# Attention over pooled keys and a gated MLP on one core: exp, pooling and filler products of the first phase rearranged

## The chip, the core and the metric

One core of a Trainium2 chip runs the whole program. Its engines are TensorE (PE, matrix products; PEld is its weight load), VectorE (DVE), ScalarE (ACT), GpSimd (POOL) and SyncE (SP), which here only issues transfers. Each engine works through its own instruction list in order and waits on semaphores. The metric is the device time of one execution in microseconds (us); the time before is the median of three.

## The reference

For each of 8 batches and 8 heads (576 tokens, 64 numbers a head) keys and values are averaged over groups of 8 tokens, so that 72 are left; then softmax attention, and the heads side by side are the rows x of a gated MLP:

```python
k_p = k.reshape(B, H, Sp, pool, D).mean(axis=3)      # Sp = 72, pool = 8
v_p = v.reshape(B, H, Sp, pool, D).mean(axis=3)
scores = scale * np.matmul(q, k_p.transpose(0, 1, 3, 2))
attn = np.exp(scores - np.max(scores, axis=-1, keepdims=True))
attn = attn / (np.sum(attn, axis=-1, keepdims=True) + 1e-09)
x = heads side by side of np.matmul(attn, v_p)       # 4608 x 512
xn = x / rms * rms_g                                 # rms over the 512
g = xn @ w_gate; val = xn @ w_val                    # 512 x 1536 each
out = (g * sigmoid(g) * val) @ w_out                 # 1536 x 512
```

The weights come as 64-bit numbers; the kernel converts them itself.

## The kernel before

Heads are taken in pairs (p = 0 to 3 in each batch b), tokens of the MLP in 9 blocks of 512, the 1536 inner columns in 12 pieces f. A 32-bit number is split into a high and a low part of a shorter format, and a product of two numbers is made of three: high by high, high by low, low by high. So a block needs 12 x 36 = 432 products of 128 x 128 by 512.

**The later phase** (blocks 1 to 8) is plain code: while PE works on block i, the attention of the batch after it is made a step at a time. Its first step takes the first pair of batch 2: k is loaded, summed over the groups by DVE (`s_kpool`), and only then q, since both use one buffer; then `s_heads` makes the scores.

**The first phase** makes batches 0 and 1, converts all weights, and runs block 0. Its order is the string `ORDER`: each word is a step with its indices, called in turn, and so the order of every engine's list. The steps that matter here, with the letter in the string: k, q, v load a pair; K and V sum keys and values over groups on DVE; S makes a pair's scores `pss` (two heads, five tiles each); M takes the row maxima of a head and multiplies them by minus the scale; E makes the exponentials, five ACT instructions for a head with the sum of a row as a second result; R makes the inverse of the sums; N multiplies on POOL; T transposes on PE into `pst`, C and D copy that (DVE, ACT); A is the product with the values, `psx`, X and Y copy it (DVE, ACT); Z squares it, P sums squares by PE (`psr`), p adds those up (`total`), r takes the root, s the inverse, B spreads it (`psb`), I makes the scaled x, x and y its high and low part (`xh`, `xl`). l loads a piece of weights, a (ACT), b, c, d (DVE: shift, `w_low`, sign) convert it, h (ACT) and w or W (DVE or POOL) split it. g and e are the gate and value products of a piece f (`mm1`, tile `psg`), G, F, i, j or L the steps between (`gate` on ACT, `val` on DVE, `act_hi` on ACT, `act_lo` on DVE or POOL), o the output products (`mm2`, tile `po`). z is `warm`, 16 products of the identity with itself, once, at the start.

The split of block 1's x (`split_x(1)`: for each of four pieces two ACT and two DVE instructions) follows behind the string. The last output products of block 0 copy their result to `o`, and SP sends it out; k and v of batch 2 stand behind those in SP's list.

## Time and profile before

| | |
|---|---|
| time, median of 3 runs (range) | 1046.81 us (1045.53 to 1047.74) |
| profiled execution, and its span | 1049.04 us, 1047.3 us |
| PE busy, products | 1026.6 us, 98% |
| DVE, ACT, POOL busy | 506.3, 416.6, 115.9 us (48%, 40%, 11%) |
| mean granted clock of TensorE | 0.98 of full (full is 2.4 GHz, 0.5 is 1.2 GHz) |

The time of the profiled execution is 1.7 us more than its span, which goes from the first to the last instruction. PE counts as busy from a product's start to its modelled end, also when it runs at half clock, so the shares are read stretch by stretch.

### The profile page before, as it was taken

The page shows a single profiled execution, that of the slowest core. Times are in us where ns is not written, and L with a number is a line of the kernel's source. Part 1 is how long each engine was busy: PE and PEld are TensorE (multiplying, and loading weights), DVE is VectorE, ACT ScalarE, POOL GpSimd, SP SyncE. Part 2 cuts the span into 40 slices and gives each one's busy share as a digit, 9 for nine tenths or more (in the row PEclk, how much of TensorE's full clock was granted, in tenths as well). Part 3 has the DMA queues.
Part 4 walks back from the last instruction along what each step waited for, and adds up shares of the span by engine and source line. Part 5 has one row for each costly group of instructions (what it writes and reads, how often), then busy time and mean ns, then how long its engine had stood idle before and what let it go on. Part 6 is the DMA issues. An engine that isn't in the chain of part 4 may idle for free.

```text
span 1047.3 us, 13134 instructions
## 1 busy us (share of the span) xinstructions
PE 1026.6 (98%) x4994; PEld 816.2 (78%) x4994; DVE 506.3 (48%) x857; ACT 416.6 (40%) x771; POOL 115.9 (11%) x108
## 2 busy tenths in 40 slices
PE   7899998999999999999999999999999999999998
PEld 6677776777877777777877787778777888888886
DVE  6799985635455446344653455445452431122112
ACT  5767664433443345333533354335342431121111
POOL 2313430111001100111001101110011000000000
PEclk8599999999999999999999999999999999999999
DMA  9445412222022201221122103210210010001001
GB/s 292 133 163 177 170 62 72 74 76 74 25 73 73 58 25 50 77 66 36 43 75 54 57 3 108 55 53 12 88 36 14 1 41 1 1 1 41 1 1 40
DMA packets 38702, 65.44 MB, mean 62 GB/s; under 512 B 6384, under 2 KB 20208, under 8 KB 37360
## 3 DMA queue, kind: packets, MB, share of 16 engines
q1 hardware_dynamic: 38640, 64.61, 20.3%
q8 instruction: 39, 0.64, 0.3%
q14 instruction: 23, 0.19, 0.1%
HBM read 47.19 MB, written 9.44 MB: 54 GB/s over the span
## 4 chain that ended last, share of the span: by engine, by line
PE 88%; DVE 5%; DMA 2%; ACT 2%; issue 1%; SPq 0%; ACTq 0%
PE psg L490 53%; PE po L521 27%; PE pss L282 4%; PE psx L343 3%; DVE wt L140 1%; DMA wx<-w 1%; DVE wt L144 1%; DMA main<-kT 1%; DVE wt L136 1%; ACT prob L260 1%; PE psr L412 1%; DVE w L162 0%; PE pst L323 0%; PE psb L436 0%; DMA q<-qT 0%
## 5 line engine op out<-in xcount | busy, mean ns | idle before, releaser
L490 PE MATMUL psg<-xh,w 128*128 128x512 f32 x1728 | 541.3, 395 | 2.9 <-ACT xh L462 2.9
L490 PEld LDWEIGHTS psg<-xh,w 128*128 128x128 f32 x1728 | 322.3, 189 | 82.9 <-ACT xraw L350 3.4
L490 PE MATMUL psg<-xl,w 128*128 128x512 f32 x864 | 338.2, 392 | 0.0
L521 PE MATMUL po<-w,hh 128*128 128x512 f32 x864 | 223.3, 395 | 0.0
L502 DVE TENSOR_TENSOR act<-act,psg 128x512 f32<-128x512 f32 x108 | 73.6, 682 | 288.1 <-PE psg L490 254.5
L521 PEld LDWEIGHTS po<-w,hh 128*128 128x128 f32 x864 | 162.6, 188 | 37.7
L490 PEld LDWEIGHTS psg<-xl,w 128*128 128x128 f32 x864 | 162.6, 188 | 35.5 <-DVE xl L463 0.7
L506 ACT CAST hh<-act 128x512 fp32r<-128x512 f32 x108 | 67.1, 622 | 212.5 <-DVE act L502 212.4
L497 ACT ACTIVATE act<-psg 128x512 f32<-128x512 f32 x108 | 64.5, 597 | 204.8 <-PE psg L490 202.6
L521 PE MATMUL po<-w,hl 128*128 128x512 f32 x432 | 122.4, 395 | 0.4 <-DVE hl L510 0.4
L521 PEld LDWEIGHTS po<-w,hl 128*128 128x128 f32 x432 | 79.5, 188 | 20.3 <-DVE act L502 2.0
L510 DVE TENSOR_TENSOR hl<-act,hh 128x512 fp32r<-128x512 f32 x102 | 70.0, 686 | 40.9 <-ACT hh L506 38.5
L299 POOL TENSOR_TENSOR prob<-prob,sm 128x360 f32<-128x360 f32 x48 | 38.7, 826 | 446.2 <-DVE sm L297 257.9
L497 ACT ACT_TABLE_LOAD x40 | 51.3, 1283 | 47.8 <-PE psg L490 26.6
L291 DVE TENSOR_REDUCE mx<-pss 128x5 f32<-128x360 f32 x48 | 23.4, 528 | 49.8 <-PE pss L282 49.6
L304 DVE STREAM_TRANSPOSE sq<-prob 128x960 f32<-128x960 f32 x24 | 28.3, 1179 | 38.8 <-POOL prob L299 34.6
L384 POOL TENSOR_TENSOR acc<-acc,sq 128x576 f32<-128x576 f32 x21 | 30.7, 1461 | 146.4 <-ACT sq L378 146.4
L239 DVE TENSOR_REDUCE pv<-v 72x128 f32<-72x1024 f32 x28 | 34.0, 1214 | 22.8 <-PE psx L343 21.5
L282 PEld LDWEIGHTS pss<-pk,q 64*128 64x128 f32 x560 | 34.5, 193 | 12.0 <-issue 8.9
L282 PE MATMUL pss<-pk,q 64*128 64x72 f32 x560 | 38.6, 283 | 1.8 <-DVE own L329 0.9
L294 ACT ACTIVATE prob<-prob 128x360 f32<-128x360 f32 x48 | 23.1, 505 | 31.9 <-DVE prob L293 31.8
L343 PE MATMUL psx<-pt,pv 72*64 72x256 f32 (+2 forms) x224 | 35.4, 429 | 0.0
(90 smaller groups left out, 701.2 us busy)
## 6 DMA issues: line engine op xcount, KB each, us to landing
wx<-w SPq DMA_DIRECT2D x10, 1024.0 KB
v<-vN SPq DMA_DIRECT2D x32, 288.0 KB
out<-o SPq DMA_DIRECT2D x36, 256.0 KB
wx<-w SPq DMA_DIRECT2D x16, 512.0 KB
k<-kT SPq DMA_DIRECT2D x28, 288.0 KB
q<-qT SPq DMA_DIRECT2D x28, 288.0 KB
pt<-sq SPq DMA_DIRECT2D x96, 40.0 KB
pt<-sq SPq DMA_DIRECT2D x96, 32.0 KB
```

The source lines that it names most:

```text
L239: nc.vector.tensor_reduce(pv, s["v"], AX.X, ALU.add)
L282: nc.tensor.matmul(s["ps", h][:, t * SP:(t + 1) * SP], s["q"][r, o:o + P], s["pk"][r, :], start=True, stop=True)
L299: nc.gpsimd.tensor_tensor(pr, pr, sm[:, :, None].broadcast_to(shape), ALU.mult)
L304: nc.vector.transpose(sq.rearrange("p b g j -> p g b j"), prob.rearrange("p g (b j) -> p g b j", b=3))
L343: nc.tensor.matmul(ps[r, :n], s["pv"][:, r], s["pt"][:, h, tok], start=True, stop=True)
L384: nc.gpsimd.tensor_add(acc[b], acc[b], st[b, p]["sq"])
L490: nc.tensor.matmul(ps[:, :NB], w[:, c, cols], x[c], start=(j == 0), stop=(j == len(todo) - 1))
L497: nc.scalar.activation(t, ps[:, :NB], AF.Silu)
L502: nc.vector.tensor_mul(t, t, ps[:, :NB])
L506: nc.scalar.copy(a, st["act"])
L510: eng.tensor_sub(l, st["act"], hh[i, f].bitcast(F32))
L521: nc.tensor.matmul(po[i][t], x[i, f][:, t * P:(t + 1) * P], w, start=(f == 0 and k == 0), stop=(f == NF - 1 and k == 2))
```

## The change

- `warm` multiplies `ones` (the short format) by itself, into one fixed bank. It stands at three places: 35 products at the start, 5 behind the first scores, 28 ahead of the first `psb`.
- The values of batch 0 are loaded in another layout (`v0`, tokens down) and summed over groups by five products with a 0/1 matrix `group` (`s_vpool0`, `psv`), then copied once. The four DVE sums of batch 0's values go.
- Four of the eight sums of keys in the first phase go to POOL, as three adds each (step %).
- For 12 of the 16 early heads the exponentials are made as in the later phase: DVE subtracts the maximum (u), ACT makes the exponentials of the whole head in one instruction (f), DVE sums (n). The other four heads keep E; for those pairs ACT multiplies the pooled keys by minus the scale (~), so that M is one minimum. The product of the maximum with the scale goes for all 16.
- For batch 1 the sums of both heads are scaled by ACT and inverted in one instruction.
- `ORDER` is another string; which steps of the weights and the activations go to POOL changes with it (w and W, j and L).
- `split_x(1)` (step O) stands in the string, ahead of the last `val`.

```diff
-zg:0 k01 q00 k00 v00 q01 v01 q02 k02 v03 K01 v02 k03 q03 l3 l1 l0 K00 l2 l5 S00:01 V00 k10 q10 S01:45 M000 M001 E000
+zz k01 k00 q00 q02 k02 q01 U0 U1 q03 K01 U2 k03 l3 %00 l0 l1 l5 l2 ~00 k10 S00:01 q10 K02 M001 z5 S02:45 M000 E001
...
-Fa B11:1 H10 ia o9 H11 gb:2 La eb:3 Gb oa Fb ib jb ob k20 v20
+ea:3 Ga bo co hp do wp ho o9 Fa Wo ia gb:2 La eb:3 Gb oa O1 Fb ib jb ob k20 v20
...
+    group = const.tile([P, 2 * SP - 8], F32, name="group")
+    nc.vector.memset(group, 0.0)
+    nc.vector.tensor_reduce(group[:, 64:80], ident.rearrange("p (s o) -> p s o", o=POOL), AX.X, ALU.add)
...
+    def load_v0(i):
+
+        if i < 2:
+            v = st["v0", i] = space2(NF - 1 - i, [P, 2, DM], F32, f"v0_{i}")
+            nc.sync.dma_start(v, v0[i * 2 * P:(i + 1) * 2 * P].rearrange("(t p) n -> p t n", p=P))
+        else:
+            v = st["v0", 2] = space2(NF - 3, [P, 2, DM], F32, "v0_2")
+            nc.sync.dma_start(v[:S - 4 * P, 0, :], v0[4 * P:])
+
+    def s_vpool0(t):
+
+        if t == 0:
+            st["pv0"] = bank(0, "psv")
+        n = min(P, S - t * P)
+        nc.tensor.matmul(st["pv0"][:SP, :], group[:n, 64 - 16 * t:64 - 16 * t + SP], st["v0", t // 2][:n, t % 2, :],
+                         start=(t == 0), stop=(t == 4))
...
+        if pool:
+            for w in (4, 2):
+                nc.gpsimd.tensor_add(k[:, :, :w], k[:, :, :w], k[:, :, w:2 * w])
+            nc.gpsimd.tensor_add(pk, k[:, :, 0], k[:, :, 1])
+        else:
+            nc.vector.tensor_reduce(pk, k, AX.X, ALU.add)
...
+    def s_negate(b, p):
+
+        st[b, p]["neg"] = True
+        nc.scalar.mul(st[b, p]["pk"], st[b, p]["pk"], -EXP_SCALE)
...
-        nc.vector.tensor_reduce(mx, s["ps", h][:, :n * SP].rearrange("p (t k) -> p t k", k=SP), AX.X, ALU.max)
-        nc.vector.tensor_scalar(mx, mx, -EXP_SCALE, None, ALU.mult)
+        nc.vector.tensor_reduce(mx, s["ps", h][:, :n * SP].rearrange("p (t k) -> p t k", k=SP), AX.X,
+                                ALU.min if "neg" in s else ALU.max)
...
+    def s_less(b, p, h):
+
+        s, n = st[b, p], len(OFFS2)
+        nc.vector.tensor_tensor(
+            probs(b, p, h), s["ps", h][:, :n * SP].rearrange("p (t k) -> p t k", k=SP),
+            s["mx"][:, h, :, None].broadcast_to([P, n, SP]), ALU.subtract)
+
+    def s_plain(b, p, h):
+
+        pr = probs(b, p, h)
+        nc.scalar.activation(pr, pr, AF.Exp, scale=EXP_SCALE)
+
+    def s_sum(b, p, h):
+        nc.vector.tensor_reduce(st[b, p]["sm"][:, h, :], probs(b, p, h), AX.X, ALU.add)
...
-        ps = bank(0, "warm")
         for _ in range(n):
-            nc.tensor.matmul(ps[:, :P], ident, ident, start=True, stop=True)
+            nc.tensor.matmul(st["warm"][:, :P], ones, ones, start=True, stop=True)
 
     with tc.manual_schedule(engines=ENGINES):
         first_phase()
-        split_x(1)
```

Where it moves instructions: PE's list between the last sums of squares and the first gate product, before (`pst`, `psx` of batch 1's first pair around `psb`) and then of the change.

```order
L412 MATMUL psr_339<-one,own_119 116x1 x5
L323 MATMUL pst_0_0_494<-ident,prob 72x128 x4
L436 MATMUL psb_0_505<-ident,r_491 128x116 x3
L436 MATMUL psb_0_505<-ident,r_491 128x112
L436 MATMUL psb_0_505<-ident,r_491 128x52
L436 MATMUL psb_1_517<-ident,r_491 128x64
L323 MATMUL pst_0_2_520<-ident,prob 72x128 x2
L323 MATMUL pst_0_1_524<-ident,prob 72x128 x4
L343 MATMUL psx_0_0_541<-pt_0_493,pv_0_438 64x288 x2
L343 MATMUL psx_0_1_550<-pt_0_493,pv_0_438 64x288 x2
L490 MATMUL psg_0_0_564<-xh_0_546,w_0_384 128x512 x2
```

```order
L473 MATMUL psr_364<-one,own_176 116x1 x5
L656 MATMUL warm<-ones 128x128 x28
L497 MATMUL psb_0_551<-ident,r_508 128x116 x3
L497 MATMUL psb_0_551<-ident,r_508 128x112
L497 MATMUL psb_0_551<-ident,r_508 128x52
L497 MATMUL psb_1_561<-ident,r_508 128x64
L384 MATMUL pst_0_0_565<-ident,prob 72x128 x4
L384 MATMUL pst_0_1_578<-ident,prob 72x128 x4
L384 MATMUL pst_0_2_587<-ident,prob 72x128 x2
L343 MATMUL pss_1_0_591<-pk_1_457,q_1_472 128x72
L343 MATMUL pss_1_1_592<-pk_1_457,q_1_472 128x72
```

The filler products stand ahead of `psb`. Behind the last row come eight more scores of the second pair (`pss_1`) and then `psg`; `psx` of the first pair stands behind the first gate product's twelve.

DVE's list at the end of block 0, before and of the change: `act_11` is `val(11)`, `hl_11` its low part, `xl` the low parts of block 1's x.

```order
L502 TENSOR_TENSOR act_11_1509<-act_11_1509,psg_11_1_1496 128x512
L510 TENSOR_TENSOR hl_11_1526<-act_11_1509,hh_11_1524 128x512
L527 COPY o_0_1531<-po_0_656 128x512
L527 COPY o_2_1543<-po_2_658 128x512
L463 SCALAR_TENSOR_TENSOR xl_0_1560<-xraw_297,gcol,xh_0_1556 128x64
L463 SCALAR_TENSOR_TENSOR xl_0_1560<-xraw_540,gcol,xh_0_1556 128x448
L463 SCALAR_TENSOR_TENSOR xl_1_1561<-xraw_297,gcol,xh_1_1557 128x64
```

```order
L563 TENSOR_TENSOR act_10_1473<-act_10_1473,psg_10_1_1460 128x512
L524 SCALAR_TENSOR_TENSOR xl_0_1545<-xraw_340,gcol,xh_0_1541 128x64
L524 SCALAR_TENSOR_TENSOR xl_0_1545<-xraw_638,gcol,xh_0_1541 128x448
L524 SCALAR_TENSOR_TENSOR xl_1_1546<-xraw_340,gcol,xh_1_1542 128x64
L524 SCALAR_TENSOR_TENSOR xl_1_1546<-xraw_638,gcol,xh_1_1542 128x448
L524 SCALAR_TENSOR_TENSOR xl_2_1547<-xraw_340,gcol,xh_2_1543 128x64
L524 SCALAR_TENSOR_TENSOR xl_2_1547<-xraw_638,gcol,xh_2_1543 128x448
L524 SCALAR_TENSOR_TENSOR xl_3_1548<-xraw_340,gcol,xh_3_1544 128x64
L524 SCALAR_TENSOR_TENSOR xl_3_1548<-xraw_638,gcol,xh_3_1544 128x448
L563 TENSOR_TENSOR act_11_1527<-act_11_1527,psg_11_1_1514 128x512
L571 TENSOR_TENSOR hl_11_1568<-act_11_1527,hh_11_1566 128x512
L588 COPY o_0_1573<-po_0_717 128x512
```

The eight `xl` stood behind the copies of the output and now stand ahead of `val(11)`.

DVE's list at the first maxima, of the change: `sm` rows are sums and their inverse.

```order
L281 TENSOR_REDUCE mx_2_216<-pss_2_1_187 128x5
L298 TENSOR_TENSOR main_131<-pss_2_1_187,mx_2_216 128x360
L281 TENSOR_REDUCE mx_2_216<-pss_2_0_186 128x5
L298 TENSOR_TENSOR main_131<-pss_2_0_186,mx_2_216 128x360
L281 TENSOR_REDUCE mx_1_225<-pss_1_1_205 128x5
L298 TENSOR_TENSOR main_126<-pss_1_1_205,mx_1_225 128x360
L322 TENSOR_SCALAR sm_0_179<-sm_0_179 128x5
L323 RECIPROCAL sm_0_179<-sm_0_179 128x5
L281 TENSOR_REDUCE mx_1_225<-pss_1_0_204 128x5
L298 TENSOR_TENSOR main_126<-pss_1_0_204,mx_1_225 128x360
L308 TENSOR_REDUCE sm_2_217<-main_131 128x5
L322 TENSOR_SCALAR sm_2_217<-sm_2_217 128x5
```

Before, each maximum was followed by its product with the scale, and there was neither the subtraction into `main` nor a sum on DVE.

## Rows read from the trace of the kernel before

**Rows 1.** The page's first line.

```profile
span 1047.3 us, 13134 instructions
```

**Rows 2.** Busy time by engine in stretches: start:end, length, then PE, PEld, DVE, ACT and POOL busy us with instruction counts, mean granted clock of TensorE (1 is full), DMA share, GB/s. The first stretch goes from the first row maximum to the last of the four `first_x` products, the second from there to the last piece of converted weights.

```profile
9.56:52.95 43.39, 36.33 (x217) 26.84 (x217) 34.69 (x78) 33.39 (x138) 13.82 (x13) 0.62 0.65 211
52.95:161.20 108.25, 103.56 (x511) 80.47 (x511) 102.24 (x136) 72.33 (x150) 35.75 (x22) 0.98 0.41 138
```

**Rows 3.** The chain of work that ended last, in order of time, some pieces of 0 to 190 us: start, length, what (x: instructions in the piece).

```profile
22.52 1.52 ACT main L260 x10
...
35.79 4.04 PE psx L343 x16
39.83 5.91 PE psr L412 x30
...
45.76 0.18 DVE total L417
...
47.82 2.82 PE psb L436 x12
...
55.12 12.12 PE psg L490 x48
...
182.37 4.02 DMA q<-qT
...
186.52 1.34 PE pss L282 x20
```

**Rows 4.** The view of Rows 2, one microsecond to a row; the third figure from the end is the granted clock.

```profile
12.00:13.00 1.00, 0.00 (x0) 0.00 (x0) 0.23 (x2) 0.64 (x6) 0.00 (x0) 0.94 1.08 242
...
57.00:58.00 1.00, 1.00 (x5) 0.82 (x4) 0.96 (x3) 0.98 (x3) 0.03 (x1) 0.88 0.63 168
...
180.00:181.00 1.00, 1.00 (x4) 0.77 (x3) 1.00 (x5) 0.95 (x3) 0.00 (x0) 0.56 1.01 301
```

**Rows 5.** Instructions in order of time in 0 to 60 us: start, length, engine, line, operation, tiles, count; in brackets the idle time before it and what ended it.

```profile
1.35 6.07 PE L593 MATMUL warm<-ident 128*128 128x128 f32 x32 [1.35 <-POOL ident masks.py:199]
...
9.56 0.52 DVE L248 TENSOR_REDUCE mx<-pss 128x5 f32<-128x360 f32 x1
...
18.39 2.41 PE L282 MATMUL pss<-own,main 64*128 64x72 f32 x20
...
20.73 2.35 PE L323 MATMUL pst<-ident,main 128*72 128x128 f32 x10
...
28.43 1.07 POOL L272 TENSOR_TENSOR main<-main,sm 128x360 f32<-128x360 f32 x1 [0.39 <-ACT own L329]
...
52.78 1.14 ACT L474 CAST xh<-xraw 128x512 fp32r<-128x512 f32 x2
```

**Rows 6.** The same view of PE later, at the full clock.

```profile
88.36 1.07 PE L323 MATMUL pst<-ident,prob 128*72 128x128 f32 x8 [0.38 <-POOL prob L272]
...
95.12 1.19 PE L343 MATMUL psx<-pt,pv 72*64 72x288 f32 x8
...
155.42 1.08 PE L412 MATMUL psr<-one,acc 128*116 128x1 f32 x10
```

**Rows 7.** Groups of instructions by line and shape: total busy us, mean ns of one, idle time before them. ACT's is from the page; the next five are DVE's of 0 to 55 us; the last two are DVE's of 188 to 1000 us, where the later phase subtracts the maximum and sums in instructions of their own.

```profile
L294 ACT ACTIVATE prob<-prob 128x360 f32<-128x360 f32 x48 | 23.1, 505 | 31.9 <-DVE prob L293 31.8
...
L239 DVE TENSOR_REDUCE own<-v 72x128 f32<-72x1024 f32 x4 | 4.8, 1204 | 1.7 <-DMA v<-vN 1.7
...
L329 DVE COPY own<-pst 72x512 f32<-72x512 f32 x5 | 3.3, 666 | 0.3 <-PE pst L323 0.3
L228 DVE TENSOR_REDUCE own<-main 128x72 f32<-128x576 f32 x4 | 3.0, 749 | 4.8 <-DMA main<-kT 4.8
...
L249 DVE TENSOR_SCALAR mx<-mx 128x5 f32<-128x5 f32 x10 | 1.8, 184 | 0.3
...
L356 DVE COPY xraw<-psx 128x288 f32<-128x288 f32 x1 | 0.5, 456 | 1.0 <-ACT own L361 1.0
...
L293 DVE TENSOR_TENSOR prob<-pss,mx 128x360 f32<-128x360 f32 x48 | 23.7, 522 | 0.0
...
L296 DVE TENSOR_REDUCE sm<-prob 128x5 f32<-128x360 f32 x48 | 23.0, 521 | 0.3
```

**Rows 8.** The same view of DVE: the weights' step `w_low` at 1024 columns, in 0 to 55 us and in 55 to 182 us.

```profile
L140 DVE SCALAR_TENSOR_TENSOR wt<-wx,wt 128x1024 uint32<-128x1024 uint32 x1 | 1.2, 1215 | 0.0
...
L140 DVE SCALAR_TENSOR_TENSOR wt<-wx,wt 128x1024 uint32<-128x1024 uint32 x9 | 16.5, 1828 | 0.2
```

**Rows 9.** Who PE waited for in 55 to 190 us: total us, times, longest us.

```profile
PE psg L490 <- ACT xh L462: 2.9, 1, 2.9
PE pst L323 <- POOL prob L272: 2.4, 2, 2.0
```

**Rows 10.** Instructions of all engines in order of time at the end of block 0 and the start of block 1.

```profile
170.25 0.69 DVE L502 TENSOR_TENSOR act<-act,psg 128x512 f32<-128x512 f32 x1 [5.90 <-PE psg L490]
...
172.75 0.40 PE L521 MATMUL po<-w,hl 128*128 128x512 f32 x1
...
177.66 3.30 ACT L462 ACTIVATE xh<-xraw,gcol 128x64 fp32r<-128x64 f32 x8
...
178.16 0.46 SPq L200 DMA_DIRECT2D k<-kT  x1
178.59 3.08 DVE L463 SCALAR_TENSOR_TENSOR xl<-xraw,gcol,xh 128x448 fp32r<-128x448 f32 x7 [0.27 <-ACT xh L462]
```

More of the change, by code (lines that the diff above doesn't have):

```diff
@@ L72 @@
+F8 hk wi i8 Wk B10:0 bn B11:1 H10 g9:2 H11 j8 e9:3 cn G9 bm dn cm lp hn o8 dm F9 lo hm wn i9 wm ga:2 j9 ap bp cp ao dp
+ea:3 Ga bo co hp do wp ho o9 Fa Wo ia gb:2 La eb:3 Gb oa O1 Fb ib jb ob k20 v20
 """
@@ L76, in body @@
 @with_exitstack
-def body(ctx: ExitStack, tc: tile.TileContext, qT, kT, vN, w1, w2, gain, out):
+def body(ctx: ExitStack, tc: tile.TileContext, qT, kT, vN, v0, w1, w2, gain, out):
     nc = tc.nc
@@ L219, in load_v, with s_vcopy0, s_kpool @@
         nc.sync.dma_start(v, vN[b, p])
-    def s_kpool(b, p):
+    def load_v0(i):
[11 more added lines that the diff above has]
+                         start=(t == 0), stop=(t == 4))
+    def s_vcopy0():
+        pv = st["v0", 2][:SP, 1, :]
+        nc.scalar.copy(pv, st["pv0"][:SP, :])
+        for p in range(NP):
+            st.setdefault((0, p), {})["pv"] = pv[:, p * P:(p + 1) * P]
+    def s_kpool(b, p, pool=False):
         s = st[b, p]
@@ L247, in s_max @@
         mx = s["mx"][:, h, :]
-        nc.vector.tensor_reduce(mx, s["ps", h][:, :n * SP].rearrange("p (t k) -> p t k", k=SP), AX.X, ALU.max)
-        nc.vector.tensor_scalar(mx, mx, -EXP_SCALE, None, ALU.mult)
-    def s_exp(b, p, h):
-        s, n = st[b, p], len(OFFS2)
-        if b == 0:
-            pr = main(p)[:, 2 * S:].rearrange("p (g k) -> p g k", k=SP)
-        else:
-            pr = prob[:, :, :SP]
-        s["pr", h] = pr = pr[:, h * n:(h + 1) * n, :]
-        for t in range(n):
-            nc.scalar.activation(pr[:, t, :], s["ps", h][:, t * SP:(t + 1) * SP], AF.Exp, scale=EXP_SCALE,
+        nc.vector.tensor_reduce(mx, s["ps", h][:, :n * SP].rearrange("p (t k) -> p t k", k=SP), AX.X,
+                                ALU.min if "neg" in s else ALU.max)
@@ new lines, in probs @@
+    def probs(b, p, h):
+        s, n = st[b, p], len(OFFS2)
+        if ("pr", h) not in s:
+            if b == 0:
+                pr = main(p)[:, 2 * S:].rearrange("p (g k) -> p g k", k=SP)
+            else:
+                pr = prob[:, :, :SP]
+            s["pr", h] = pr[:, h * n:(h + 1) * n, :]
+        return s["pr", h]
+    def s_less(b, p, h):
+        s, n = st[b, p], len(OFFS2)
+        nc.vector.tensor_tensor(
+            probs(b, p, h), s["ps", h][:, :n * SP].rearrange("p (t k) -> p t k", k=SP),
+            s["mx"][:, h, :, None].broadcast_to([P, n, SP]), ALU.subtract)
@@ L261, in s_exp, with s_inverse @@
+    def s_plain(b, p, h):
[3 more added lines that the diff above has]
+        nc.vector.tensor_reduce(st[b, p]["sm"][:, h, :], probs(b, p, h), AX.X, ALU.add)
+    def s_exp(b, p, h):
+        s = st[b, p]
+        pr = probs(b, p, h)
+        for t in range(len(OFFS2)):
+            nc.scalar.activation(pr[:, t, :], s["ps", h][:, t * SP:(t + 1) * SP], AF.Exp, scale=-1.0,
                                  bias=s["mx"][:, h, t:t + 1], accum_out=s["sm"][:, h, t:t + 1])
-    def s_inverse(b, p, h):
-        sm = st[b, p]["sm"][:, h, :]
-        nc.vector.tensor_scalar(sm, sm, float(POOL), POOL * 1e-9, ALU.mult, ALU.add)
+    def s_inverse(b, p, h=None):
+        sm = st[b, p]["sm"] if h is None else st[b, p]["sm"][:, h, :]
+        if h is not None:
+            nc.vector.tensor_scalar(sm, sm, float(POOL), POOL * 1e-9, ALU.mult, ALU.add)
@@ L267, in s_inverse, with s_eight @@
         nc.vector.reciprocal(sm, sm)
+    def s_eight(b, p):
+        sm = st[b, p]["sm"]
+        nc.scalar.activation(sm, sm, AF.Copy, scale=float(POOL), bias=POOL * 1e-9)
     def s_norm(b, p, h, eng):
@@ L580, in first_phase @@
             i=lambda f: act_hi(0, f), j=lambda f: act_lo(0, f, V), L=lambda f: act_lo(0, f, G), o=lambda f: mm2(0, f),
-            z=warm)
+            z=warm, O=split_x, U=load_v0, t=s_vpool0)
+        steps.update({"+": s_vcopy0, "%": lambda b, p: s_kpool(b, p, True), "~": s_negate, "&": s_eight})
+        st["warm"] = psum.tile([P, 512], F32, tag="bank2", name="warm")
         nc.sync.dma_start(gcol, gain)
```

48 lines of the change are left out of this document (22 added, 26 removed).

## Prediction

> **What bounds the kernel now.** I read the busy times by stretch first, then the chain that ended last, then the single instructions at the places where the chain changes engines. After 188 us PE does nothing but products back to back, from code that the change leaves alone: about 859 of the span's 1047.3 us [rows 1]. What can move is when PE gets there. Four stretches lead to it.
>
> A, up to the first product with weights at 55.12 us [rows 3]: softmax of batch 0. Between the first row maximum at 9.56 and the last `first_x` at 52.95, PE is busy for 36.3, DVE for 34.7 and ACT for 33.4 of 43.4 us, at a mean clock of 0.62 [rows 2]. No engine is full; they wait for each other in turn, and DVE stands idle for 43.4 - 34.7 = 8.7 us. The clock fell near the end of the 13th microsecond, with PE idle, and came back in the 58th, two us into the dense products [rows 4]. In between the chain goes over PE at half clock: 16 `psx` in 4.04 us, 30 `psr` in 5.91, 12 `psb` in 2.82 [rows 3]. At full clock 8 `psx` take 1.19, 10 `psr` 1.08 and 8 `pst` 1.07 [rows 6].
>
> B, from there to 161 us: PE is busy for 103.6 of 108.3 us, DVE for 102.2 [rows 2]: DVE has only 6.0 us to spare. C, the seam between blocks: PE waits 2.9 us for the new block's `xh` [rows 9], falls to half clock [rows 4], and `pss` of the first later pair starts at 186.52, when its q lands 4.15 us after the issue [rows 3].
>
> **The change, term by term (start of steady work, minus is earlier).**
>
> *DVE's work in A stays.* Removed there: four sums of values at 1.20 and two of keys at 0.75, ten products of the maximum at 0.18, and seven copies or small steps that go to ACT, about 2.9 (five copies at 0.67 become one and two short ones): 11.0 us. Added: eight subtractions at 0.52, eight sums at 0.52, three copies at 0.46 and some 1.9 us of weight work that now stands ahead: 11.6 us [rows 7]. So A can gain from idle time alone, 8.7 us at most. ACT is relieved: five exponentials of a head with their reads take 1.52 [rows 3], one for the whole head 0.505 [rows 7], for eight heads 8 us less.
>
> *PE in A.* With the values' sums gone from DVE, the eight normalizations on POOL, whose last ended at 29.5 [rows 5], end near 24.5 by my count: POOL sums the fourth pair's keys between the first normalization and the second (three adds, some 1.5 us; bounds 1.07 and 3.2, one and three normalizations [rows 5]), whose transfer is now batch 0's last; I put the end of that at 17.2, and seven normalizations of about 1.0 follow. That leaves PE. From the end of the fourth pair's `pss` (20.7 before [rows 5], about 19.0 after) it has 36 `pst`, 32 `psx`, 40 `psr`, 20 `pss` to do. At half clock this is 8.5 + 8.1 + 7.9 + 2.4 = 26.9 us, at full 4.8 + 4.8 + 4.3 + 1.3 = 15.2 [rows 3, 5, 6]. Before needed 24.9, waits included. The sum of squares `total` (45.76 [rows 3]) so comes at 39.5 at best (9.56 plus DVE's 29.9 without a wait) and at 19.7 + 26.9 = 46.6 at worst. I take 43.5, nearer to the worst because PE has half clock in most of A and the new products are few: 35 at the start in place of 16 of two passes each, 5, and 28. **-2.3.**
>
> *The 28 products before `psb`* stand where PE waited 2.06 us (45.73 to 47.82 [rows 3]). The old ones took 6.07 us for 32 passes [rows 5], 0.19 each, and 0.11 is a `psr` pass at full clock [rows 6]: 3.1 to 5.3 us. So they outlast the wait by 1.0 to 3.2: **+1.6**, as the clock may rise on the way. If it does, `psb` and its first product gain about 0.9, and block 0's first eight products, at half clock before, 1.1: **-2.0**. Last, `psx` of batch 1's first pair goes behind the first gate product; before, `xh` was ready at 53.92 [rows 5] and PE came at 55.12: **-1.2**. Its 1.2 us come back in B, but the 1.34 us of the second pair's `pss` leave it.
>
> *B.* PE waits 2.4 us for normalized rows [rows 9]. A pair's two exponentials shrink from 3.0 to 1.0 us, so I take **-2.0**, between +1.5 (a new wait as long as that) and -4.6 (all that PE is idle, 108.3 - 103.6). DVE hides this only just: its weight steps and POOL's compete. POOL gets 12 adds for keys and three more 1024-column pieces, and loses two of 512 and three `act_lo`.
>
> *C.* `split_x(1)` now stands ahead of `val(11)` on DVE and `act_hi(11)` on ACT. From the first `xh` to the last `xl` it takes 4.0 us (177.66 to 181.67 [rows 10]), and it can start when the first two of the last twelve gate products are through, about 167.8. So `val(11)` starts at 171.8 by the old times instead of 170.25, and `mm2(11)`, which began at 172.75 [rows 10], waits 1.1 to 1.55 us. Its outputs, then k (issued 5.4 us after that start, behind four output transfers in SP's queue), then q, all go by it; DVE takes k up to 0.5 us sooner, since `split_x` no longer stands before it. `pss` comes **+1.0** later against the old order, and the dense products that now start early only wait there: 12 and 24 of 0.23 us end 8.3 us after `mm2(11)` starts, `pss` follows at 13.3. PE idles 5 us. After 2.9 us it fell to half clock [rows 4, 9]; then `pss` takes 2.41 instead of 1.34 [rows 3, 5]: **+1.2** (0 to 2).
>
> What costs nothing: the transfers of batch 0's values have the same 1.15 MB. The 35 products start an us later than the old (they need `ones`) and end near 8.2, about when k is ready; the first maximum stands behind a sum of keys on DVE either way.
>
> Sum: -2.3 + 1.6 - 2.0 - 1.2 - 2.0 + 1.0 + 1.2 = -3.7. Against the profiled execution (1049.04, of which 1.7 lie around the span) that is 1045.3; that execution is 2.2 above the median 1046.81, so **1043.1 for the median**.
>
> **Rivals.**
>
> 1. *The clock stays up through A.* For it: fewer idle us between products. Then `total` comes near 42, the 28 products end with the wait, and the first weight product starts at 50: -5.1, with 1.1 and 2.0 as above and +2.2 in C: -6.0, 1040.8; with all waits of B gone 1038.2. Against it: before, PE was busy for 36 of 43 us and had a mean clock of 0.62.
>
> 2. *PE at half clock sets the pace.* `total` at 46.6 (+0.8), the 28 products +3.2, the rest as forecast (-2.0, -1.2, -2.0, +2.2): +1.0, 1047.8; with half of the 3.2 it is 1046.2. For it: DVE's and ACT's relief reaches PE at nothing if PE is the one that is late. So the change would not do what its first part says.
>
> 3. *The other side: DVE loses to POOL in A and B.* In 55 to 182 us `w_low` at 1024 columns takes 1.83 us in the mean, 1.22 where it ran alone [rows 8]. Three more 1024-column pieces on POOL at 0.6 to 1.2 each and six us of key adds at half of that would cost DVE 5 to 6.6 us. That eats the 5.9 us that stretches A and B give, and C's +2.2 is left: 1049.0. It decides from 6 us of added DVE time on. Against it: DVE has 8.7 + 6.0 us idle. The Trainium skill ("SBUF — State Buffer", section "Who interferes with whom") says that a DVE instruction with two SBUF inputs and a GpSimd instruction that reads SBUF take turns, and the later one blocks fully; the trace's 1.83 against 1.22 us agrees with it, and by it alone this rival would be the forecast.
>
> **How the numbers follow.** Forecast 0.44, rival 1 0.22, rival 2 0.19, rival 3 0.15. 0.2% is 2.1 us, about what this measurement can tell from no change. The forecast alone spans 1041 to 1045.5, of which I count 0.37 as faster by more than that and 0.07 as within; rival 1 is faster; rival 2 within, with 0.03 slower and 0.01 faster; rival 3 slower, but for 0.02. Faster 0.60, same 0.24, slower 0.16. The range is 1038.6 to 1047.9: below it 0.05 of rival 1, above it most of rival 3 and some of rival 2.
>
> **What would show it.** Right: the first weight product starts at 51 to 53 us at full clock; DVE's idle time from the first maximum to `first_x` falls under 7 us with its busy time within 1 us of 34.7; `mm2(11)` waits for `hl` 1 to 1.6 us; PE idles near 5 us before the first later `pss`. Wrong: `psr` still at 0.2 us a pass with `total` after 45; `w_low` above 2 us; PE waiting in B for weights; or a seam without the idle time.

## The result, and the profile after

The changed kernel takes 1056.66 us (median of 4, 1055.15 to 1057.16) against 1047.28 us of the kernel before beside it: ratio 1.0088, interval 1.0068 to 1.0107, 9.4 us slower where 3.7 faster was forecast. The profiled execution shown here has 1055.15 us, the fastest of the four, and a span of 1053.3; that of before 1047.3 [rows 1]. So 6.0 us have to be found in these two traces; a second trace of the changed kernel ("again" below) has a span of 1056.8, 9.5 more than before.

Busy time by stretch, columns as in [rows 2]; from the first row maximum to the last `first_x`, and on to the last weights:

```profile
12.51:60.21 47.70, 43.44 (x259) 34.09 (x261) 35.32 (x76) 28.26 (x70) 19.98 (x22) 0.76 0.53 184
60.21:161.20 100.99, 98.74 (x498) 77.16 (x499) 98.46 (x124) 64.17 (x109) 35.27 (x19) 0.99 0.40 131
```

DVE's is the third busy time of a row. The first stretch starts 2.95 us later than before and is 4.3 longer. DVE's work in it is 35.3 against 34.7, as forecast; its idle time is 12.4 against 8.7, of which 4.88 are one wait for PE (below).

The chain that ended last, start, length and what, pieces of 0 to 63 us:

```profile
2.39 7.73 PE warm L656 x35
10.12 2.34 PE pss L343 x20
12.46 1.26 PE warm L656 x5
13.72 4.48 PE pss L343 x40
18.19 4.75 PE psv L238 x8
...
43.37 5.89 PE psr L473 x30
49.26 6.08 PE warm L656 x28
55.34 2.56 PE psb L497 x12
...
60.03 1.97 PE pss L343 x20
62.00 1.13 PE psg L551 x4
```

All three groups of fillers lie on it, 15 us of the first 55. A filler takes 7.73 / 35 = 0.22 us. The first 20 scores, before and then in the changed kernel:

```profile
7.48 1.34 PE L282 MATMUL pss<-own,main 64*128 64x72 f32 x20
```

```profile
10.05 2.41 PE L343 MATMUL pss<-own,main 64*128 64x72 f32 x20
```

They start 2.6 us later and take 2.41, the time of half clock [rows 5], where they took 1.34. Behind `psr` the 28 fillers run on for 6.1 us, while what `psb` needs is long ready:

```profile
49.30 0.18 DVE L478 TENSOR_REDUCE total<-psr 116x5 f32<-116x20 f32 x1 [2.32 <-PE psr L473]
...
50.60 0.18 DVE L488 RECIPROCAL r<-r 116x5 f32<-116x5 f32 x1
...
55.14 2.76 PE L497 MATMUL psb<-ident,r 116*128 116x116 f32 x12
...
57.49 2.72 DVE L530 SCALAR_TENSOR_TENSOR xraw<-xraw,gcol,psb 128x512 f32<-128x512 f32 x4 [4.88 <-PE psb L497]
```

`psb`'s input is there at 50.78, `psb` starts at 55.14, and DVE loses 4.88 us. From the sum of squares to `psb` it is 5.84 us; before 2.06 [rows 3].

The seam, instructions in order of time and the wait:

```profile
173.69 1.07 PE L582 MATMUL po<-w,hl 128*128 128x512 f32 x4
...
177.76 0.50 PE L582 MATMUL po<-w,hl 128*128 128x512 f32 x1 [1.14 <-DVE hl L571]
...
190.53 1.86 PE L343 MATMUL pss<-pk,q 64*128 64x72 f32 x20 [4.27 <-DMA q<-qT]
```

Start by start: the first gate product 55.05 to 61.93 (+6.9); from there to the output products of piece 10 114.92 to 111.76 (-3.2); to the first later scores 16.55 to 16.84 (+0.3); from there to the end 860.78 to 862.77 (+2.0). Sum +6.0. In the second trace the same four are +8.3, -3.0, +0.6 and +3.6, 9.5 in all, as the medians ask.

### The profile page after: what moved, and what is told of

It reads as the page before. It is cut to its first block, busy times and chain, and to the rows that moved or that the text cites. A ratio compares the mean times of both kernels' runs of the same rounds, so it can differ in the third digit from the quotient of the medians.

```text
span 1053.3 us, 13126 instructions
## 1 busy us (share of the span) xinstructions
PE 1034.7 (98%) x5040; PEld 825.5 (78%) x5040; DVE 504.9 (48%) x852; ACT 405.2 (38%) x667; POOL 124.4 (12%) x118
## 4 chain that ended last, share of the span: by engine, by line
PE 88%; DVE 6%; DMA 2%; issue 2%; ACT 2%; POOL 0%; SPq 0%; ACTq 0%; DVEq 0%; POOLq 0%
PE psg L551 51%; PE po L582 26%; PE pss L343 4%; PE psx L404 3%; PE warm L656 1%; DVE wt L145 1%; DVE wt L149 1%; DVE wt L141 1%; DMA wx<-w 1%; PE psr L473 1%; PE psv L238 1%; DVE act L563 1%; DVE w L167 1%; ACT wt L137 0%; DVE hl L571 0%
## 5 line engine op out<-in xcount | busy, mean ns | idle before, releaser
L524 DVE SCALAR_TENSOR_TENSOR xl<-xraw,gcol,xh 128x64 fp32r<-128x64 f32 (+7 forms) x60 | 26.7, 496 | 20.2 <-ACT xh L523 17.8
```

## The experiments

Each run's ratio is to the kernel before on the same chip and at the same time, 0.1% is 1.05 us. The runs were spread over four chips, so a difference of two ratios is often one between chips.

| run | median us | ratio to before [95%] |
|---|---|---|
| changed kernel, again | 1058.00 | 1.0092 [1.0069, 1.0115] |
| no fillers | 1048.25 | 0.9985 [0.9974, 0.9996] |
| without the 28 | 1051.67 | 1.0028 [1.0017, 1.0040] |
| wide fillers for the 28 | 1053.95 | 1.0047 [1.0032, 1.0062] |
| split's place undone | 1051.93 | 1.0025 [1.0011, 1.0039] |
| no fillers, split undone | 1043.93 | 0.9955 [0.9937, 0.9973] |
| identity start, no 5, no 28 | 1045.10 | 0.9966 [0.9953, 0.9978] |
| full-precision ones at the start, no 5, no 28 | 1045.88 | 0.9970 [0.9958, 0.9982] |
| identity start, split undone | 1041.52 | 0.9932 [0.9920, 0.9944] |
| that, with the old exponentials | 1065.60 | 1.0169 [1.0144, 1.0193] |
| identity start, new split, early k | 1039.43 | 0.9918 [0.9905, 0.9931] |
| before + 35 of ones at the start | 1050.76 | 1.0011 [1.0002, 1.0021] |
| before + the 28 | 1054.59 | 1.0041 [1.0027, 1.0056] |
| before + the split's new place | 1053.14 | 1.0035 [1.0020, 1.0049] |
| before + split's new place + early k | 1048.28 | 0.9985 [0.9973, 0.9997] |
| before + new exponentials | 1056.95 | 1.0067 [1.0051, 1.0082] |

The profiled executions, start by start (us): when the sum of squares `total` starts; from it to the first gate product; on to the output products of piece 10; from those to the end.

| run | `total` at | to first gate product | to piece 10's output | to the end |
|---|---|---|---|---|
| before | 45.76 | 9.29 | 114.92 | 877.3 |
| changed | 49.30 | 12.63 | 111.76 | 879.6 |
| changed, again | 51.13 | 12.25 | 111.94 | 881.5 |
| without the 28 | 49.07 | 7.59 | 111.70 | 881.4 |
| wide fillers for the 28 | 51.15 | 10.05 | 111.68 | 881.6 |
| split's place undone | 47.89 | 11.07 | 113.15 | 876.9 |
| no fillers | 46.56 | 8.44 | 111.80 | 879.7 |
| no fillers, split undone | 44.07 | 8.15 | 111.81 | 877.2 |
| identity start | 41.96 | 8.08 | 111.79 | 881.7 |
| identity start, split undone | 42.48 | 7.92 | 111.84 | 877.1 |
| identity start, new split, early k | 40.52 | 8.09 | 111.54 | 875.3 |
| before + the 28 | 47.60 | 13.71 | 115.14 | 877.0 |
| before + split's new place | 46.35 | 9.30 | 116.31 | 882.0 |
| before + split's new place + early k | 46.73 | 9.30 | 116.38 | 875.9 |

Up to `total` the five rows from "changed" to "split's place undone" run the same code, and it comes at 47.89 to 51.15: executions differ there by 3.3 us without any edit. (The granted clock differs too: its first fall is in the 32nd us in the second trace of the changed kernel, in the 38th in the first.) Without fillers it comes at 44.07 and 46.56, with the identity start at 40.52 to 42.48, so the three kinds of start don't overlap; but a single trace can't be read to better than some 3 us in this stretch.

My theory from the first two traces was that the fillers delay what stands behind them and give no clock back; the rival, that they pay for themselves and the loss is the seam's.

### Fillers out: all, and the 28 alone

```diff
-zz k01 k00 q00 ... M001 z5 S02:45 ... R10 zs B00:0
+k01 k00 q00 ... M001 S02:45 ... R10 B00:0
```

> All three groups of filler products are left out; the rest is the changed kernel. Theory 1 (the fillers stand in PE's own list and delay what is behind them, and they give no clock back): the first row maximum comes 2.5 to 3.3 us earlier than in the changed kernel (12.51, so 9.2 to 10.0), the first gate product 6 to 8 us earlier (61.9, so 54 to 56), the time is 6 to 9 us below the changed kernel's, 1047.5 to 1050.5. Theory 2 (the fillers cost about what they give, and the loss comes from the seam and from half clock in the rest): the first gate product moves by less than 2.5 us, the time by less than 3.

> Only the 28 filler products ahead of psb are left out. Theory 1: psb starts at about 51.5 in place of 55.14 (the end of psr plus the 2.1 us that the sum, the root and the inverse take), the first gate product and the time are 3 to 4 us earlier, 1052.5 to 1053.5; the clock stays at half through psb with or without them. Rival (the 28 raise the clock in time for the gate products): the first eight gate products go at half clock without them, and 1.1 of that is given back, so that the time falls by 2 or less.

> The changed kernel itself, unchanged, beside the other experiments on one chip, so that their differences to it can be read. Expected from the earlier runs: 6 to 9.5 us above the kernel before.

Without any the time is 1.6 us below the kernel before, so it falls by 1.0092 - 0.9985 = 1.07%, 11.2 us: more than I took, and the rival falls. Without any filler:

```profile
6.95 6.68 PE L343 MATMUL pss<-own,main 64*128 64x72 f32 x60 [6.95 <-ACT own L267]
...
46.56 0.18 DVE L478 TENSOR_REDUCE total<-psr 116x5 f32<-116x20 f32 x1 [2.79 <-PE psr L473]
...
48.19 2.79 PE L497 MATMUL psb<-ident,r 116*128 116x116 f32 x12 [1.66 <-DVE sm L323]
...
55.00 2.11 PE L551 MATMUL psg<-xh,w 128*128 128x512 f32 x8
```

The scores start as soon as their keys are there, at 6.95; `psb` follows the sum by 1.63; and the first eight gate products take 2.11, the full clock, as in the changed kernel with the 28:

```profile
61.93 2.12 PE L551 MATMUL psg<-xh,w 128*128 128x512 f32 x8
```

The forecast had credited that to the fillers. They don't even secure it: with the split undone and the fillers kept the same eight take 3.42. The 28 alone: from the sum to `psb` 1.61 in place of 5.84, so 4.2 us are shown; the medians say 6.7 (1.0092 - 1.0028), with an interval of some 2.7 to either side and between two chips. Ahead of the edit `total` comes 0.2 us earlier in this trace than in the first of the changed kernel, 2.1 earlier than in the second.

### The 28 in the kernel before

```diff
-s0 R101 B00:1
+s0 R101 zs:2 B00:1
```

(with the ones for z's products there, the identity for the start's.)

> The kernel before with the 28 filler products of the short format ahead of psb and nothing else. As in the changed kernel they should take 6.2 us at half clock against a wait of 2.06 (from the sum of squares to psb 5.84 in place of 2.06) and not raise the clock: 3.5 to 4.2 us above the kernel before. Rival: the denser work behind them raises the clock for block 0's first eight products (3.12 to 2.1): 2.5 to 3 above.

Measured 1.0041, 4.3 us. `psb` starts 6.53 after the sum in place of 2.06, and the first eight gate products still take about what they took before (first line), 3.36:

```profile
55.05 3.12 PE L490 MATMUL psg<-xh,w 128*128 128x512 f32 x8
```

```profile
48.12 6.21 PE L594 MATMUL warm<-ones 128*128 128x128 f32 x28
54.13 2.76 PE L436 MATMUL psb<-ident,r 116*128 116x116 f32 x12
...
61.31 3.36 PE L490 MATMUL psg<-xh,w 128*128 128x512 f32 x8
```

So the price holds in both orders, and nothing comes back; the rival falls.

### Wider fillers in their place

```diff
-R10 zs B00:0
+R10 zc B00:0
...
+            if n == 12:
+                nc.tensor.matmul(st["warm"], ones, ones[:, None, :].broadcast_to([P, 4, P]), start=True, stop=True)
```

> The changed kernel with 12 products of 512 columns of the same ones in place of the 28 of 128 columns ahead of psb; all else stays. At half clock 12 take 5.2 us (0.43 each), about what the 28 took. If the width decides (wide products raise the clock, 28 short ones of 0.22 did not): the 12 end in under 4.5 us, psb takes 1.6 in place of 2.76, the transposes and scores behind it 1.3 in place of 2.3 and 2.0, and the time falls 2 to 4 us below the changed kernel's. If no filler raises the clock here: within 1 us of the changed kernel.

```profile
50.98 5.47 PE L657 MATMUL warm<-ones 128*128 128x512 f32 x12
56.24 1.66 PE L497 MATMUL psb<-ident,r 116*128 116x116 f32 x12
57.73 1.26 PE L384 MATMUL pst<-ident,prob 128*72 128x128 f32 x10
59.64 1.34 PE L343 MATMUL pss<-pk,q 64*128 64x72 f32 x20 [0.65 <-ACT pt L390]
```

The 12 took 5.47, not less than 4.5: the granted clock (third figure from the end, one row a microsecond) rises at their end only.

```profile
55.00:56.00 1.00, 1.00 (x4) 0.81 (x3) 0.00 (x0) 0.12 (x1) 0.92 (x2) 0.50 0.63 106
56.00:57.00 1.00, 1.00 (x8) 0.90 (x6) 0.00 (x0) 0.00 (x0) 0.47 (x1) 0.67 0.77 258
57.00:58.00 1.00, 1.00 (x12) 1.00 (x11) 0.30 (x1) 0.00 (x0) 0.00 (x0) 1.00 0.40 160
```

But it rises, from half (1.2 GHz) to full (2.4), and all that follows goes at full clock. So at the same place, after the same work, 28 products of 128 columns (6.2 us) didn't raise it and 12 of 512 (5.5 us) did. From the sum of squares to the first gate product it is 10.05 us, against 12.63 with the 28 and 7.59 without them. The time is 1.0047 against 1.0092, 4.7 us less where 2 to 4 were expected; it stays above 1.0028, the version without the 28, though hardly beyond the intervals, and clearly above 0.9985, that without any.

### What stands at the start

Three kernels: the 35 of ones in the kernel before; the identity start in the changed kernel; and the ones as full precision there, which have the numbers of the one and the format of the other.

```diff
-zg:0 k01
+zz:0 k01
...
-nc.tensor.matmul(ps[:, :P], ident, ident, start=True, stop=True)
+nc.tensor.matmul(ps[:, :P], ones, ones, start=True, stop=True)
```

> The kernel before, with 35 filler products of the ones in place of its 16 of the identity at the start, and nothing else. Theory 1: the first scores start at about 10.1 at half clock, the first maximum at 11.8 to 12.5 in place of 9.56, and the time is 1.5 to 3 us above the kernel before, since no engine of this phase has slack to take the delay back but some of PE's and DVE's waits. Rival (the first phase waits for transfers and takes a late start back): within 0.7 us.

```diff
-zz k01 k00 q00 ... z5 ... zs
+zg k01 k00 q00 ...
...
-nc.tensor.matmul(st["warm"][:, :P], ones, ones, start=True, stop=True)
+nc.tensor.matmul(st["warm"][:, :P], ident, ident, start=True, stop=True)
```

> The changed kernel with the start of the kernel before (16 products of the full-precision identity, 32 passes) in place of the 35 of ones, and without the other two groups; the split stays in its new place. Theory A (it is the kind of the product that decides whether the clock is full when the first scores come): the first scores start at about 7.5 at full clock (1.34 for 20), the first maximum at 8.9 in place of 12.51, psv takes 2.5 to 3 in place of 4.8; the time is 1 to 3 us below the version without any filler (1048.25), 1045 to 1047. Theory B (at the start nothing but the length counts, or the gain is lost behind): within 1 us of the version without fillers.

```diff
-nc.tensor.matmul(st["warm"][:, :P], ident, ident, start=True, stop=True)
+nc.tensor.matmul(st["warm"][:, :P], ones.bitcast(F32), ones.bitcast(F32), start=True, stop=True)
```

> As the version with the identity start and the split in its new place (1045.1), but the 16 products at the start are of the ones read as full precision, two passes each, so that only the numbers in them differ. If the format decides (a full-precision product, two passes of 0.19 each, raises the clock and one of the short format does not): the rate rises within the start, the first scores take 1.3 to 1.5 us for 20 and start about 1 us later than with the identity (8.1), the time is 0 to 2 us above it. Rival (the numbers decide: mostly zeros raise the clock, ones do not): the first scores go at half clock, 2.41, and the time is 3 to 5 us above it.

Passes of the filler by microsecond (PE's busy time and count in brackets, then the granted clock), first the changed kernel, then the full-precision ones:

```profile
3.00:4.00 1.00, 1.00 (x7) 1.00 0.98 362
...
6.00:7.00 1.00, 1.00 (x7) 1.00 1.00 348
7.00:8.00 1.00, 1.00 (x7) 1.00 1.01 370
```

```profile
3.00:4.00 1.00, 1.00 (x6) 1.00 1.03 359
...
6.00:7.00 1.00, 1.00 (x9) 1.00 0.92 332
7.00:8.00 1.00, 1.00 (x11) 1.00 1.01 366
8.00:9.00 1.00, 0.15 (x2) 1.00 1.02 392
```

The short format stays at 6 or 7 a microsecond to the end; the same ones read as full precision begin at that rate and end at 11, and then 20 scores take 1.34, as in the kernel before. Theory A holds, and at 128 columns the format decides and not the numbers: 1.0028 with the 35 and the 5, 0.9966 with the identity (6.5 us), 0.9970 with full-precision ones. Of the 6.5, 4.5 come from leaving the short products out (1.0028 - 0.9985, on one chip) and 2.0 more from the identity. The five products share in the 4.5; they weren't taken alone. With the identity the whole first stretch moves: the last normalization of batch 0 on POOL ends at 23.96, the sum of squares is at 41.96, the first gate product at 50.04.

In the kernel before the 35 cost only 1.2 us (1.0011), less than I expected. Its trace shows the scores 2.7 later, but the sum of squares at 47.60, which another execution with the old start has as well ("before + the 28"). Why the old order loses less, I did not test. In the changed kernel PE has the values' sums too, ten passes; the first eight here and with the identity start:

```profile
18.12 4.82 PE L238 MATMUL psv<-v,group 128*72 128x512 f32 x8
```

```profile
11.27 3.62 PE L238 MATMUL psv<-v,group 128*72 128x512 f32 x8
```

In the changed kernel the first three start 0.92, 0.86 and 0.73 us before the next, the next four 0.43: the rate rises only here, near 20 us. With the identity start it is 0.46 and then 0.42 to 0.43 from the first on. I took this for the reason that the changed kernel loses more, but it isn't shown: with the identity start and the split undone the clock falls in the 12th microsecond, the eight take 5.21, and `total` still comes at 42.48.

### The split's new place

```diff
-gb:2 La eb:3 Gb oa O1 Fb ib jb ob k20 v20
+gb:2 La eb:3 Gb oa Fb ib jb ob k20 v20
...
         first_phase()
+        split_x(1)
```

> The changed kernel, with the split of block 1's x back behind the last output products. By the prediction's term (+2.2 for the split's new place and the clock behind it) the time falls by 2.2. By what the trace of the changed kernel shows (from the first of the last output products to the first later scores 16.84 us, before 16.55, and 1.5 for half clock behind): by 0 to 2; but the 2.9 us that PE then waits for the split come back, and only the wait for q gets shorter, so I take a fall of 1.0.

> Both suspects undone: no filler products, and the split of block 1's x back behind the last output products. If the fillers and the seam are the whole loss and add up: from the first of the last output products to the first later scores 16.1 us, from there to the end 860.8, so the profiled span is 2.5 to 3.5 below that of the version without fillers alone (1046.5), 1043 to 1044, and the time 3 to 4 us below the kernel before (what stretch B gained, 3.1). Rival (what the split's new place costs is only moved elsewhere): no more than 1 us below the version without fillers alone.

> The kernel before with one change: the split of block 1's x ahead of the last val. By the traces (from the last output products but one to the first later scores 0.2 to 0.8 us longer, and 2.1 from there to the end, where the clock falls in the wait for q) 2.3 to 2.9 us above the kernel before; the difference of the medians with and without fillers gave 3.1 and 6.7. If 6.7 holds, there is a cost that the traces didn't show.

(The last one puts the split ahead of the last val in the kernel before, the reverse of the edit above.)

The new place costs 3.7 us alone in the kernel before; 3.1 in the changed one without fillers (0.9985 - 0.9955), 3.6 with the identity start (0.9966 - 0.9932). In its trace in the kernel before PE waits 4.30 us for q:

```profile
190.11 2.15 PE L282 MATMUL pss<-pk,q 64*128 64x72 f32 x20 [4.30 <-DMA q<-qT]
```

With the fillers it came out as 7.0 (1.0092 - 1.0025, two chips); the trace of that run shows 2.7 there (16.08 in place of 16.84, 860.81 in place of 862.77), 4.6 against the second trace of the changed kernel. The rest lies ahead of the first gate product (58.96 in place of 61.93 and 63.38; 1.2 to 1.4 of that is given back behind it), where this edit changes nothing: in the traces that is the spread between executions, not a cost of the split. The 7.0 has an interval of some 2.8 to either side; of the changed kernel six executions were timed for it, from 1054.95 to 1060.34.

### k early

```diff
-eb:3 Gb oa O1 Fb ib jb ob k20 v20
+eb:3 Gb k20 v20 oa O1 Fb ib jb K20 ob
...
-        steps.append(lambda: (pool_k(first), pool_v(first)))
+        steps.append(lambda: pool_v(first))
```

(First with the identity start; then the same edit together with the split's new place in the kernel before.)

> The identity start, no other fillers, the split of block 1's x in its new place ahead of the last val; besides, k and v of batch 2's first pair are issued ahead of the last two groups of output products instead of behind the output transfers, and k's sum stands on DVE behind the last act_lo, so that q is issued 5 to 10 us sooner. If the wait for q (4.4 in the version with the identity start) is what the new place of the split turns PE's idle time into: no wait there, the first later scores 8.3 us after the last output products start, the clock stays full behind it (860.8 to the end in place of 862.8), and the span is about 1037, 1 to 3 us below the version with the seam back. Rival (the transfers of k and v collide with the last weights, or DVE's sum delays the outputs): no better than the version with the seam back.

> As that, and k and v of batch 2's first pair issued ahead of the last two groups of output products, k's sum behind the last act_lo, as in the fastest version. The wait for q goes, and with it the idle time of the seam: 1.5 to 3 us below the kernel before (the first later scores 12.4 us after the last output products but one in place of 16.55, of which about 3.6 were useful products of block 1 in either case... so by the fastest version's trace, from those output products to the end 1035.4 - 160.16 = 875.2 in place of 877.3).

```profile
164.23 0.50 PE L582 MATMUL po<-w,hl 128*128 128x512 f32 x1 [1.15 <-DVE hl L571]
172.66 1.34 PE L343 MATMUL pss<-pk,q 64*128 64x72 f32 x20
...
182.70 1.34 PE L343 MATMUL pss<-pk,q 64*128 64x72 f32 x20 [0.27 <-DMA q<-qT]
...
193.99 0.76 PE L404 MATMUL psx<-pt,pv 72*64 72x320 f32 x4 [0.92 <-PE psx L404]
```

The first wait for q is gone: the scores come 8.43 after the last output products start, where it took 12.77 in the changed kernel, at full clock. With the split undone PE waits 2.9 for `xh` instead [rows 9]; here it waits 1.15 for `hl`. A part is lost again behind the scores, where PE waits 0.27 for the next q and 0.92 ahead of the next pair's `psx`: from the first later scores to the end it takes 862.8, not the 860.8 that were expected. From piece 10's output to the end 875.3 are left, against 877.1 with the split undone. 0.9918 is the fastest of all, 9 us below the kernel before; the difference to 0.9932 is within the intervals. In the kernel before the edit turns +3.7 into -1.6 (1.0035 to 0.9985), with 875.9 in place of 882.0 from piece 10's output to the end. So the loss of the seam is the wait for q and the clock behind it, not the split itself. What the early k gives alone, with the split in its old place, was not run.

### Start and split together

The edits of "identity start" and of "split's place undone".

> The changed kernel with the identity start of the kernel before, without the other two groups of fillers, and with the split of block 1's x back behind the last output products. If the start and the seam add up: first gate product at about 50.0, from it to the last output products but one (the tile of piece 10) 111.8, then 16.1 to the first later scores and 860.8 to the end, together a span of 1038.7; the time 7.5 to 9.5 us below the kernel before. Rival (an earlier start is lost at a later wait): no lower than 1043.9, the version with only the seam back and no fillers.

1041.52, 7.1 us below: the gains add up. The span is 1039.4 (expected 1038.7).

### The exponentials

```diff
+        if "neg" not in s:
+            nc.vector.tensor_scalar(mx, mx, -EXP_SCALE, None, ALU.mult)
...
-            u=s_less, f=s_plain, n=s_sum,
+            u=lambda *a: None, f=s_exp, n=lambda *a: None,
```

> As the run with the identity start and the seam back, but the exponentials of all early heads are made the old way (the product of the maximum with the scale on DVE, then five ACT instructions a head with the sum as second result; no subtraction and no sum on DVE). If the exponential in one instruction is what gains in stretch B and helps in A: from the first gate product to the last output products but one 113 to 115 in place of 111.8, and the time 2 to 4 us above the run that it is beside. Rival (DVE's 1.04 us a head less make up for ACT's 1.0 more): within 1 us, or faster.

```diff
-        nc.vector.tensor_scalar(mx, mx, -EXP_SCALE, None, ALU.mult)
...
-        for t in range(n):
-            nc.scalar.activation(pr[:, t, :], s["ps", h][:, t * SP:(t + 1) * SP], AF.Exp, scale=EXP_SCALE,
-                                 bias=s["mx"][:, h, t:t + 1], accum_out=s["sm"][:, h, t:t + 1])
+        nc.vector.tensor_tensor(
+            pr, s["ps", h][:, :n * SP].rearrange("p (t k) -> p t k", k=SP),
+            s["mx"][:, h, :, None].broadcast_to([P, n, SP]), ALU.subtract)
+        nc.scalar.activation(pr, pr, AF.Exp, scale=EXP_SCALE)
...
+        nc.vector.tensor_reduce(sm, st[b, p]["pr", h], AX.X, ALU.add)
```

> The kernel before, in its old order and with its old fillers, but the exponentials of all early heads made the new way: DVE subtracts the maximum, one ACT instruction for the head, DVE sums (ahead of the inverse); the product of the maximum with the scale is gone. DVE gets 16 heads times 0.86 us more, ACT 16 times about 1.0 less. If ACT's exponentials hold the path by themselves: 2 us or more below the kernel before. If DVE, which has 8.7 and 6.0 us idle in A and B, has to give the time back, and the gain needs the new order (that lets the scores' banks go early): between 1 us below and 5 us above it.

Both fall outside what I expected, the first far. The old form in the new order costs 24 us: 1.0169. PE's longest waits there in 5 to 80 us (total us, times, longest):

```profile
PE psv L238 <- ACT main L317: 7.4, 1, 7.4
...
PE psb L500 <- DVE sm L326: 5.8, 1, 5.8
PE psg L554 <- ACT prob L317: 5.7, 1, 5.7
```

Two of the three are PE waiting for a bank (a piece of the memory that its products are written to) whose scores ACT still reads, five instructions a head. In the new form DVE's subtraction is the last reader. The new form in the old order costs 7.0 us: its chain runs from 12.6 to 30.5 us over DVE almost without a gap (sums of keys and values, maxima, subtractions, sums), and up to 31 us ACT waits for the subtractions eight times, 21.7 us in all, of which 8.2 are the wait for the first:

```profile
ACT main L261 <- DVE main L258: 21.7, 8, 8.2
```

So either form exchanged alone loses. That the new one needs the values' sums off DVE and an order made for it is how I read the two traces; neither was taken alone, and the 7.1 us of the version with the identity start and the split undone are not split into parts.

## Why the prediction was wrong

To the first gate product the sum said -2.3 + 1.6 - 0.9 - 1.2 = -2.8; the trace has +6.9. The 9.7 us between, term by term:

- **The start, 5.8 us.** `total` was put at 43.5 and came at 49.30 (47.89 to 51.15 with this start). The step that failed stands under "What costs nothing": that the 35 products "end near 8.2, about when k is ready". They end at 10.1, since one takes 0.22 us and not 0.11 to 0.19: I took the price of passes of another format, and of `psr`, for them; and the scores, which start at 6.95 without fillers, were ready before either time. And they leave the clock at half, where the identity had raised it: I compared the number of products, never what raised the clock in [rows 5], where 32 passes of 0.19 in the mean are followed by 20 scores in 1.34. With the identity start the normalizations end at 23.96 (forecast 24.5; 31.03 in the changed kernel), and in the changed kernel DVE's work grew by 0.6 us, as put down: that part of the working was sound.
- **The 28, 2.2 us.** +3.8 in the trace instead of +1.6: 6.1 us at half clock, beyond even the upper bound of 5.3.
- **The clock "on the way", 0.9 of 2.0 us.** `psb` takes 2.76, at half clock as before. The other 1.1, block 0's first eight products, came (2.12 for 3.12 before), but without fillers as well: luck, not the reason given.
- **`psx` moved behind, 0.8 us.** From the start of `psb` to the first gate product 6.79 against 7.23: -0.4 where -1.2 was counted. The 20 scores of the second pair, which the forecast took off B, now stand here, 2.04 us, and were not added. Without the 28 the whole way from `total` is 7.59 in place of 9.29.
- **B, right in sum.** With the first eight products -3.1 forecast, -3.2 measured; 2.8 to 3.4 in ten of the eleven traces of the new order with its own exponentials, 1.8 in the one whose first eight take 3.42. The wait for normalized rows gave only half of it (2.4 to 1.2 us); a wait of `psb`, 0.9, went too, which the forecast did not name.
- **C, the right mechanism, rather too small.** +2.2 forecast, +2.3 in the trace shown (0.3 before the scores and 2.0 behind them, not 1.0 and 1.2), 4.2 in the second; 3.1 to 3.7 by the medians.

Two readings behind the 43.5 were wrong as well, so that it is in part luck how near it lies to what the identity start gives (40.52 to 42.48). The clock of the kernel before was not at half from the 13th to the 58th microsecond: in the 24th it is up again and falls in the 30th.

```profile
24.00:25.00 1.00, 0.79 (x6) 0.37 (x4) 0.90 (x4) 1.00 (x4) 0.39 (x1) 1.00 0.94 333
...
30.00:31.00 1.00, 1.00 (x6) 0.29 (x4) 1.00 (x3) 1.00 (x3) 0.23 (x1) 0.50 1.18 258
```

So half clock does not hold through all of A; and with the identity start `total` comes at the 42 that rival 1 named for a clock that stays up, though the clock falls twice on the way, in the 26th and the 33rd microsecond. And the worst case counts from 19.7 where the working puts the end of `pss` at 19.0; from there it would be 45.9.

Of the rivals, none happened. Rival 2, PE at half clock, is the nearest, but its worst `total` (46.6) began from an undelayed start. Rival 3 had the sign and not the mechanism: `w_low` at 1024 columns became cheaper, 1.57 us in place of 1.83 [rows 8], and DVE waited more in A; the rule that it went by (the Trainium skill, "SBUF — State Buffer", section "Who interferes with whom": such instructions of DVE and GpSimd take turns) is not refuted by that, but it was no bound in A, with 12.4 us of DVE idle, and in B, where DVE is busy for 98.5 of 101.0 us, the stretch came as forecast all the same:

```profile
L145 DVE SCALAR_TENSOR_TENSOR wt<-wx,wt 128x1024 uint32<-128x1024 uint32 x9 | 14.1, 1565 | 0.2
```

Of the signs of being right, DVE's busy time, the wait for `hl` (1.14) and PE's idle time in the seam (4.27) came as put down; the first weight product at 51 to 53 (61.93) and DVE's idle time under 7 (12.4) did not. Of the signs of being wrong, the first came in full: 30 `psr` in 5.89 us, 0.2 each, with `total` at 49.30. The range missed the time because every case in it let the start cost nothing.

What stays open: why executions of the same code differ by up to 3.3 us ahead of `total`, which is more than most of the terms above; why the 35 cost the old order so little; and what each of the other changes (values' sums on PE, keys' sums on POOL, the new order) gives by itself. The 28 and the split taken alone in the kernel before (4.3 and 3.7 by the medians) agree within the intervals with the traces of the stretches that they change (4.4 and 4.7).

## What to carry to other kernels

A filler ahead of work that is nearly ready stands on the path: price it by its own instruction form at the clock that rules there, and see in the trace that form raise the clock before counting on it. When an engine is relieved, ask which resource its instruction held (here a bank of scores), since an order made for the new holder doesn't run with the old, nor the other way about. A step moved ahead in one list may only move the idle time to the next transfer; moving the transfer's issue as well made the same move gain. And take a second trace of the same code before reading a difference of some us in one stretch.

## What the runs showed of the hardware that I had not expected

- 35 and 28 filler products of the short format, 128 columns each, went on at 0.22 us each to the end, 7.7 and 6.1 us with PE busy all the time, and PE was at half clock behind them. After the 35, the 5 and 60 scores, with PE busy from 2.4 to 18 us, it still was; it rose in the passes of 512 columns that followed. Sixteen products of the same numbers as full precision (5.8 us), and 12 products of 512 columns (5.5 us), left it at full clock. Which property of the product decides, I did not find out.
- The granted clock reads 1.00 in the first 37 us of the changed kernel, while the fillers and scores there go at half rate and the passes of `psv` then change from 1.1 to 0.59 us near 20 us. Neither the half clock at the start nor that rise is in the record, whose first change is the fall in the 38th microsecond; in the kernel before it is the fall in the 13th, though the fillers' rate had risen before it. At a program's start only the rate of the instructions tells the clock; so the mean of 0.76 for the first stretch above is too high.
